# Attention, a Mish feed-forward and a routed mixture of experts: score products of two heads in turn, one half-sequence ahead

## The chip, the cores and the metric

The kernel runs on one core of a Trainium2 chip. The metric is the device time of one launch in microseconds (us). TensorE multiplies matrices, VectorE, ScalarE and GpSimd work on elements (GpSimd is POOL in the profile, VectorE DVE, ScalarE ACT), and SyncE (SP) issues most of the DMAs. The time before is the median of three runs.

## The reference

```python
scores = scale * np.matmul(q, k.transpose(0, 1, 3, 2))   # 4 x 8 heads, 576 x 576, head size 64
scores = np.where(masks[None], scores, -1e9)              # heads 0-3: the last 32 keys
                                                          # heads 4-7: every 4th of the last 128
attn = np.exp(scores - scores.max(-1, keepdims=True))
attn = attn / (attn.sum(-1, keepdims=True) + 1e-09)
x = np.matmul(attn, v)                                    # -> 2304 tokens x 512
h = x @ w_in                                              # 512 x 2048
sp = np.where(h > 20.0, h, np.log1p(np.exp(np.minimum(h, 20.0))))
x = (h * np.tanh(sp)) @ w_out                             # Mish, 2048 x 512
# every token goes to one of 8 experts (argmax of x @ w_gate):
# out = gate_w * sigmoid(x @ w_output_gate)[e] * relu(x @ w1[e]) @ w2[e]
```

The feed-forward weights w_in and w_out arrive as 8-byte floats and are made into 4-byte floats on the chip. Products that need more than one TensorE pass of reduced precision are made from a high and a low part of each operand (hi and lo, three products).

## The kernel before

The 2304 tokens are eight half-sequences (halves) j = 0 to 7 of 288 tokens; even ones are the first half of a sequence, odd ones the second.

**Attention of a half** goes by four pairs of heads p. Queries and keys of a pair lie with the one head's 64 dimensions in partitions 0 to 63 and the other's in 64 to 127. `att_b(j, p, h)` makes the masked scores of one head h in one PSUM bank (three blocks of 96 queries x 128 keys for the near heads, four of 72 x 72 or 72 x 104 for the dilated ones; L219), takes the row maximum (L226), the exponentials with their sums (ScalarE, L229), and multiplies each block by the reciprocal of its sums (L239). `att_c` transposes the probabilities (L250) and copies them out, `att_d` multiplies them with the values of both heads, alternating (L268), and splits the result into xhi (ScalarE, L274) and xlo (VectorE, L275), the input of the feed-forward. An fp32 product counts as two passes in the trace.

**PSUM** has eight banks: `ps_acc` with four (the feed-forward's sums acc), `ps_h` with two (hps) and `ps_a` with two, in turn. For j below EARLY = 2 scores and outputs use ps_acc and only transposes ps_a; later halves use ps_a for all three. There the mask is added when VectorE takes the scores out (L225); for the first two halves TensorE writes it into the bank (L213) and the queries are scaled beforehand (L212).

**The feed-forward** runs in 128 steps g, each for one half and 128 of the 2048 inner columns: `l1` (12 products hps, L408), Mish in `mish_a` to `mish_d`, and three steps later `l2` (12 products into the four banks acc, L451). Steps 0 to 31 take halves 0 and 1 in turn, four steps each; then come 16 steps for each half. Mish is made from exp(min(h, 20)): VectorE clamps out of PSUM (L415), ScalarE takes the exponential (L416), the square is on ScalarE (L418) for g below 32 and on VectorE (L420) later, ScalarE takes a logarithm (L426) and an exponential (L427), and VectorE multiplies with h (L432). `split` writes the high part on ScalarE (L352) and subtracts it for the low part (L354).

**Weights**: of each of the 32 pieces VectorE makes 4-byte floats in three instructions (`narrow`: L343, L345, L347), then `split` follows. During steps 0 to 31 the pieces come just ahead of their use. Of the subtractions, GpSimd does those of the weights, those of glo for g below 32, and those of x2s, the routing's input (four for each half).

**Order.** The source order sets each engine's queue, with priorities that let a scheduler move work; every engine then works its queue strictly in order, waiting by semaphores. Ahead of the loop of steps stands the attention of halves 0 and 1 (`att_first`), with three short filler products (`busy`, L92) behind each operation. The attention of half j + 1 is spread over the 16 steps of half j from j = 2 on (`take`), that of half 2 from step 22. The gate weights `wg` are loaded at the start (`setup_b`) and split at step 18. After step 127 come the experts.

Of the kernel before, what the change touches and what calls it, by code (L numbers as in the profile page):

```python
# [22 lines left out]
EPS = 1e-9  # L23
# [5 lines left out]
def tile_attn_mish_moe(ctx, tc, qkv, w_in, w_out, w_gate, w_og, w1, w2, out):  # L29
# [54 lines left out]
    two5 = const.tile([128, 2], F32, name="two5")  # L84
# [24 lines left out]
    def setup_b():  # L109
# [14 lines left out]
        nc.sync.dma_start(out=wg[:, :, 0:E], in_=w_gate.rearrange("(k p) e -> p k e", p=128))  # L124
        nc.sync.dma_start(out=wg[:, :, E:2 * E], in_=w_og.rearrange("(k p) e -> p k e", p=128))
# [23 lines left out]
    EARLY = 2  # L149
# [11 lines left out]
    scq = [wp.tile([128, 4096], F32, tag="w", name="scq") for _ in range(EARLY)]  # L161
# [3 lines left out]
    def early(tag, m, *shape):  # L165

        off, size, n = dict(pr=(0, 416, 4), pt=(1664, 288, 3))[tag]
# [3 lines left out]
        names = "abc"[:len(shape)]  # L171
        return t.rearrange(f"p ({' '.join(names)}) -> p {' '.join(names)}", **dict(zip(names, shape)))
# [24 lines left out]
    def att_b(j, p, h):  # L197
# [4 lines left out]
        hp = slice(64 * h, 64 * h + 64)  # L202
        n, m, w = (3, CH, 128) if p < 2 else (DIL, NP, NP + 32 * s)
        sc = banks(j, "s", [m, n, w], "sc")
# [4 lines left out]
        first = j < EARLY  # L209
        if first:  # L210
            if h == 0:
                nc.vector.tensor_scalar(out=qT, in0=qT, scalar1=D ** -0.5, scalar2=None, op0=ALU.mult)  # L212
            nc.tensor.matmul(out=sc, lhsT=idb[0:m, 0:m], rhs=mk, start=True, stop=False, skip_group_check=True)  # L213
        for u in range(n):
            if p < 2:
                a, c = qT[hp, CH * u:CH * u + CH], kT[hp, CH * u:CH * u + 128]
            else:
                a, c = qT[hp, NP * u:NP * u + NP], kT[hp, u, 32 - 32 * s:]
            nc.tensor.matmul(out=sc[:, u, :], lhsT=a, rhs=c, start=not first, stop=True, skip_group_check=True)  # L219
        nm = ap.tile([CH, 4], F32, tag="nm", name="nm", bufs=4)  # L220
        if first:
            pr, src = early("pr", m, n, w), sc
        else:
            pr = src = ap.tile([m, n, w], F32, tag="pr", name="pr", bufs=3)
            nc.vector.scalar_tensor_tensor(out=pr, in0=sc, scalar=D ** -0.5, in1=mk, op0=ALU.mult, op1=ALU.add)  # L225
        nc.vector.tensor_reduce(out=nm[0:m, 0:n], in_=src, op=ALU.max, axis=AX.X, negate=True)  # L226
        su = ap.tile([CH, 4], F32, tag="su", name="su", bufs=4)
        for u in range(n):
            nc.scalar.activation(out=pr[:, u, :], in_=src[:, u, :], func=AF.Exp, bias=nm[0:m, u:u + 1],  # L229
                                 accum_out=su[0:m, u:u + 1])  # L230
        nc.vector.tensor_scalar(out=su[0:m, 0:n], in0=su[0:m, 0:n], scalar1=EPS, scalar2=None, op0=ALU.add)
        nc.vector.reciprocal(out=su[0:m, 0:n], in_=su[0:m, 0:n])
        for u in range(n):
            x, scale = pr[:, u, :], su[0:m, u:u + 1]
            if first and u == 3:
                nc.scalar.activation(out=x, in_=x, func=AF.Copy, scale=scale)
            else:
                eng = nc.gpsimd if (j, u) == (0, 2) else nc.vector
                eng.tensor_scalar(out=x, in0=x, scalar1=scale, scalar2=None, op0=ALU.mult)  # L239
        st["p", h] = pr  # L240

    def att_c(j, p, h):
# [6 lines left out]
        for u in range(n):
            nc.tensor.transpose(tp[:, u, :], pr[:, u, :], idn[0:m, 0:m])  # L250
        pt = early("pt", w, n, m) if j < EARLY else ap.tile([w, n, m], F32, tag="pt", name="pt")
        if h == 0:
            nc.vector.tensor_copy(pt, tp)
        else:
            nc.scalar.activation(out=pt, in_=tp, func=AF.Copy)
        st["t", h] = pt
# [669 lines left out]
    if True:  # L926
# [228 lines left out]
```

## Time and profile before

| | us |
|---|---|
| median of three runs | 872.98 (871.68 to 880.41) |
| profiled execution | 870.95 |
| its span, first to last instruction | 869.2 |
| TensorE busy | 829.0 (95%) |
| VectorE busy | 587.0 (68%) |
| ScalarE busy | 509.1 (59%) |
| GpSimd busy | 201.4 (23%) |
| first l1 product of step 32 starts | 186.4 |
| first l1 product of step 112 (last half) starts | 531.4 |
| last l2 product of the feed-forward ends | 597.2 |

Busy times of different engines lie beside one another. The share of 95% is an average: the chain of work that ended last goes through TensorE for 71% of the span, VectorE for 13%, DMA and ScalarE for 4% each. So the stretches have to be read one by one. The times of single instructions of TensorE overlap their neighbours; what a group costs is read from starts.

### The profile page before, as it was taken

Reading aid. Unit: us, or ns where it says so; the run is one execution under the profiler, and the core shown is the slowest. Engines: PE = TensorE matmul, PEld = TensorE weight load, DVE = VectorE, ACT = ScalarE, POOL = GpSimd, SP = SyncE. Lnnn points to the kernel's source line nnn. Section 1 sums busy time; section 2 is a strip of 40 time slices with the busy share of each in tenths; the row PEclk is TensorE's granted clock in tenths of the full one; section 3 lists DMA queues with packets and bytes.
Section 4 is the critical chain, followed back from the end, with each engine's and each line's share of the span. In section 5 each row is a group of like instructions: output and inputs, shape, how many; then the busy total and the mean of one; then the engine's idle time right before and its main releaser. Section 6 shows DMA issues by size and latency. Waiting matters only on the chain.

```text
span 869.2 us, 16857 instructions
## 1 busy us (share of the span) xinstructions
PE 829.0 (95%) x6151; PEld 767.1 (88%) x6151; DVE 587.0 (68%) x1630; ACT 509.1 (59%) x1427; POOL 201.4 (23%) x201
## 2 busy tenths in 40 slices
PE   7988889999999999999999999989899999999994
PEld 5877879898999999999999999889789999999993
DVE  5799898968768767777777776785484526534510
ACT  3586657876667666666666666583463525545621
POOL 3326554332101001001010110251221313123300
PEclk6899999999999999999999999999999999999998
DMA  9541548511210210120121000240684526436300
GB/s 330 180 142 56 166 163 260 157 54 30 78 43 12 67 39 29 39 66 29 31 65 39 31 28 1 85 163 22 213 276 156 194 65 227 144 135 244 121 23 18
DMA packets 39841, 91.72 MB, mean 106 GB/s; under 512 B 4643, under 2 KB 12835, under 8 KB 39756
## 3 DMA queue, kind: packets, MB, share of 16 engines
q1 hardware_dynamic: 36508, 81.16, 28.8%
q0 software_dynamic: 3248, 9.46, 3.3%
q8 instruction: 49, 0.80, 0.4%
q14 instruction: 36, 0.29, 0.1%
HBM read 73.91 MB, written 17.41 MB: 105 GB/s over the span
## 4 chain that ended last, share of the span: by engine, by line
PE 71%; DVE 13%; issue 6%; DMA 4%; ACT 4%; POOL 1%; SPq 1%; POOLq 0%; ACTq 0%; DVEq 0%
PE hps L408 20%; PE acc L451 19%; PE eh L750 8%; PE ecol L784 6%; PE sc L219 6%; DMA est<-in_moe_w_dram 3%; PE eacc L792 2%; PE o L268 2%; DVE wf L345 2%; PE tp L250 2%; DVE we L354 2%; DVE wf L343 2%; DVE wf L347 1%; ACT we L352 1%; PE busy L92 1%
## 5 line engine op out<-in xcount | busy, mean ns | idle before, releaser
L408 PE MATMUL hps<-xhi,w 128*128 128x288 f32 x1024 | 243.1, 307 | 13.5 <-DVE e L432 12.1
L408 PEld LDWEIGHTS hps<-xhi,w 128*128 128x128 f32 x1024 | 174.8, 190 | 21.2 <-DVE e L432 15.9
L451 PE MATMUL acc<-ghi,w 128*128 128x288 f32 x1024 | 171.5, 303 | 3.2 <-ACT x2T L471 2.0
L408 PE MATMUL hps<-xlo,w 128*128 128x288 f32 x512 | 153.0, 299 | 0.5
L451 PEld LDWEIGHTS acc<-ghi,w 128*128 128x128 f32 x1024 | 145.6, 190 | 8.5 <-ACT x2T L471 2.2
L750 PE MATMUL eh<-exh,we 128*128 128x256 f32 (+5 forms) x448 | 108.6, 316 | 0.0
L408 PEld LDWEIGHTS hps<-xlo,w 128*128 128x128 f32 x512 | 97.9, 191 | 2.0 <-DVE xlo L275 1.9
L352 ACT ACTIVATE we<-est 128x512 fp32r<-128x512 f32 x128 | 74.5, 624 | 39.3 <-DMA est<-in_moe_w_dram 22.6
L416 ACT ACTIVATE e<-e 128x288 f32<-128x288 f32 x128 | 55.8, 437 | 64.1 <-DVE e L415 62.1
L451 PE MATMUL acc<-glo,w 128*128 128x288 f32 x512 | 89.3, 296 | 0.0
L354 DVE TENSOR_TENSOR we<-est,we 128x512 fp32r<-128x512 f32 x92 | 69.2, 786 | 28.3 <-ACT we L352 28.1
L352 ACT ACTIVATE ghi<-e 128x288 fp32r<-128x288 f32 x128 | 56.5, 442 | 44.9 <-PE acc L451 24.4
L354 POOL TENSOR_TENSOR we<-est,we 128x512 fp32r<-128x512 f32 x36 | 49.6, 1398 | 131.2 <-ACT we L352 131.0
L426 ACT ACTIVATE e<-e,two 128x288 f32<-128x288 f32 x128 | 67.8, 530 | 20.7 <-DVE e L420 20.2
L415 DVE TENSOR_SCALAR e<-hps 128x288 f32<-128x288 f32 x128 | 57.9, 452 | 31.9 <-PE hps L408 30.5
L750 PEld LDWEIGHTS eh<-exh,we 128*128 128x128 f32 x448 | 77.1, 188 | 1.3
L451 PEld LDWEIGHTS acc<-glo,w 128*128 128x128 f32 x512 | 75.4, 189 | 0.0
L755 DVE SCALAR_TENSOR_TENSOR eg<-eh,eg 128x256 fp32r<-128x256 f32 (+5 forms) x64 | 30.9, 483 | 61.7 <-ACT eg L754 61.5
L229 ACT ACTIVATE pr<-pr,nm 96x128 f32<-96x128 f32 (+2 forms) x168 | 61.9, 370 | 16.7 <-DVE nm L226 16.5
L750 PE MATMUL eh<-exl,we 128*128 128x256 f32 (+5 forms) x224 | 69.7, 311 | 0.0
L432 DVE SCALAR_TENSOR_TENSOR e<-e,hps 128x288 f32<-128x288 f32 x128 | 56.9, 444 | 14.4 <-ACT e L427 14.1
L784 PE MATMUL ecol<-eg,we 128*128 128x440 f32 (+3 forms) x384 | 65.4, 320 | 0.5 <-DVE eg L755 0.5
(196 smaller groups left out, 1469.4 us busy)
## 6 DMA issues: line engine op xcount, KB each, us to landing
est<-in_moe_w_dram SPq DMA_DIRECT2D x64, 512.0 KB
wst<-in_moe_w_in_dram SPq DMA_DIRECT2D x16, 512.0 KB
wst<-in_moe_w_out_dram SPq DMA_DIRECT2D x16, 512.0 KB
qkv<-in_qkv_dram SPq DMA_DIRECT2D x12, 608.0 KB
qkv<-in_qkv_dram SPq DMA_DIRECT2D x14, 496.0 KB
buf<-fill SPq DMA_DIRECT2D x8, 771.0 KB
xs<-buf SPq DMA_DIRECT2D x19, 257.0 KB
scq<-in_qkv_dram SPq DMA_DIRECT2D x4, 608.0 KB
```

The costliest lines, as they stand in the source:

```text
L219: nc.tensor.matmul(out=sc[:, u, :], lhsT=a, rhs=c, start=not first, stop=True, skip_group_check=True)
L229: nc.scalar.activation(out=pr[:, u, :], in_=src[:, u, :], func=AF.Exp, bias=nm[0:m, u:u + 1], accum_out=su[0:m, u:u + 1])
L352: nc.scalar.activation(out=hi, in_=src, func=AF.Copy)
L354: eng.tensor_tensor(out=lo, in0=src, in1=hi.bitcast(F32), op=ALU.subtract)
L408: nc.tensor.matmul(out=hps[g], lhsT=w[:, a, kk, 128 * fl:128 * fl + 128], rhs=(xhi, xlo)[x][j][:, kk, :], start=(kk == 0 and n == 0), stop ...
L415: nc.vector.tensor_scalar(out=e, in0=hps[g], scalar1=20.0, scalar2=None, op0=ALU.min)
L416: nc.scalar.activation(out=e, in_=e, func=AF.Exp)
L426: nc.scalar.activation(out=r, in_=r, func=AF.Ln, scale=0.2, bias=two5[:, 1:2] if g < 2 * NF else two5[:, 0:1])
L432: nc.vector.scalar_tensor_tensor(out=u, in0=u, scalar=2.5, in1=hps.pop(g), op0=ALU.subtract, op1=ALU.mult)
L451: nc.tensor.matmul(out=accs[j][m], lhsT=w[:, a, fl, 128 * m:128 * m + 128], rhs=gg[x], start=(first and n == 0), stop=(last and n == 2))
L750: nc.tensor.matmul(out=ps, lhsT=ew[q, 0, a][:, c:c + 128], rhs=(hi, lo)[x][:, kk, 0:n], start=(k == 0), stop=(k == 3 * KD - 1))
L784: nc.tensor.matmul(out=accs["e", q][k], lhsT=ew[q, 1, a][:, c:c + 128], rhs=gg[x], start=(f == 0 and n == 0), stop=(f == NF2 - 1 and n == 2))
```

## The change

- Only half 0's attention stands ahead of the steps (EARLY = 1), with 30 and then 12 filler products behind each operation. Half 1's is taken in steps 0 to 3 and uses the two banks of ps_a for scores, transposes and outputs; its mask is still written by TensorE (PEMASK = 2).
- `att_s` makes the scores of both heads of a pair, block by block in turn, into two banks. Sums, reciprocals and the multiplication are done once for a pair; the multiplication is one VectorE instruction with two tensor operands. The scaling of the queries goes from VectorE to GpSimd.
- `split` subtracts on VectorE, but for the experts' pieces that were on GpSimd.
- Mish takes the exponential straight from PSUM; VectorE then limits it to e^20 and adds 1, from SBUF to SBUF.
- The gate weights are loaded at step 12, not at the start.

```diff
@@ setup
-        nc.sync.dma_start(out=wg[:, :, 0:E], in_=w_gate.rearrange("(k p) e -> p k e", p=128))
-        nc.sync.dma_start(out=wg[:, :, E:2 * E], in_=w_og.rearrange("(k p) e -> p k e", p=128))
-    EARLY = 2
+    EARLY = 1
+    PEMASK = 2
...
-    def att_b(j, p, h):
+    def att_s(j, p):
...
-        sc = banks(j, "s", [m, n, w], "sc")
+        sc = [banks(j, "s", [m, n, w], "sc") for _ in range(2)]
...
-        first = j < EARLY
+        first = j < PEMASK
         if first:
-            if h == 0:
-                nc.vector.tensor_scalar(out=qT, in0=qT, scalar1=D ** -0.5, scalar2=None, op0=ALU.mult)
-            nc.tensor.matmul(out=sc, lhsT=idb[0:m, 0:m], rhs=mk, start=True, stop=False, skip_group_check=True)
+            nc.gpsimd.tensor_scalar(out=qT, in0=qT, scalar1=D ** -0.5, scalar2=None, op0=ALU.mult)
+            for h in range(2):
+                nc.tensor.matmul(out=sc[h], lhsT=idb[0:m, 0:m], rhs=mk, start=True, stop=False, skip_group_check=True)
         for u in range(n):
...
-            nc.tensor.matmul(out=sc[:, u, :], lhsT=a, rhs=c, start=not first, stop=True, skip_group_check=True)
+            for h in range(2):
+                hp = slice(64 * h, 64 * h + 64)
...
+                nc.tensor.matmul(out=sc[h][:, u, :], lhsT=a, rhs=c, start=not first, stop=True, skip_group_check=True)
...
-        for u in range(n):
-            x, scale = pr[:, u, :], su[0:m, u:u + 1]
-            if first and u == 3:
-                nc.scalar.activation(out=x, in_=x, func=AF.Copy, scale=scale)
-            else:
-                eng = nc.gpsimd if (j, u) == (0, 2) else nc.vector
-                eng.tensor_scalar(out=x, in0=x, scalar1=scale, scalar2=None, op0=ALU.mult)
+        nc.vector.tensor_tensor(out=pr, in0=pr, in1=x.unsqueeze(3).to_broadcast([m, 2, n, w]), op=ALU.mult)
...
-        split(hi, lo, narrow(t) if wide else t, True)
+        split(hi, lo, narrow(t) if wide else t)
...
-        nc.vector.tensor_scalar(out=e, in0=hps[g], scalar1=20.0, scalar2=None, op0=ALU.min)
-        nc.scalar.activation(out=e, in_=e, func=AF.Exp)
+        nc.scalar.activation(out=e, in_=hps[g], func=AF.Exp)
+        nc.vector.tensor_scalar(out=e, in0=e, scalar1=math.exp(20.0), scalar2=1.0, op0=ALU.min, op1=ALU.add)
         if g < 2 * NF:
-            nc.scalar.activation(out=e, in_=e, func=AF.Square, bias=1.0)
+            nc.scalar.activation(out=e, in_=e, func=AF.Square)
         else:
-            nc.vector.scalar_tensor_tensor(out=e, in0=e, scalar=2.0, in1=e, op0=ALU.add, op1=ALU.mult)
+            nc.vector.tensor_tensor(out=e, in0=e, in1=e, op=ALU.mult)
...
-        split(hi, lo, u, g < 2 * NF)
+        split(hi, lo, u)
...
-            split(hi[:, m, :], lo[:, m, :], x2[:, m, :], True)
+            split(hi[:, m, :], lo[:, m, :], x2[:, m, :])
...
-        for i, op in enumerate(att_first()):
+        busy(30, warm, 128)
+        for i, op in enumerate(attention(0)):
             op()
-            busy(3, idb, 128)
-            if i == 4:
+            busy(12, idb, 128)
+            if i == 2:
                 setup_b()
...
-        begin = {THIRD: (2, 2 * NF)}
+        begin = {0: (1, 4), THIRD: (2, 2 * NF)}
...
+            if g == FILLS - 6:
+                nc.sync.dma_start(out=wg[:, :, 0:E], in_=w_gate.rearrange("(k p) e -> p k e", p=128))
+                nc.sync.dma_start(out=wg[:, :, E:2 * E], in_=w_og.rearrange("(k p) e -> p k e", p=128))
```

Three places of the engines' queues show what moves. The first is TensorE in the steps of the later halves: before, the two score groups of one pair of heads (sc, from the pair's loaded queries and keys qkv) stand apart, each at a place of its own between feed-forward products.

```order
L451 MATMUL acc_4676<-glo_5338,w_1800 128x288
L219 MATMUL sc_5447<-qkv_5302 96x128 x3
L408 MATMUL hps_5464<-xhi_4785,w_266 128x288
...
L451 MATMUL acc_4675<-ghi_5380,w_1800 128x288 x2
L219 MATMUL sc_5492<-qkv_5302 96x128 x3
L451 MATMUL acc_4676<-ghi_5380,w_1800 128x288 x2
```

Now a pair's six products stand together and alternate between the two banks. All pairs of halves 3 to 7 stand like this.

```order
L388 MATMUL hps_5233<-xhi_4585,w_291 128x288
L218 MATMUL sc_5251<-qkv_4589 96x128
L218 MATMUL sc_5252<-qkv_4589 96x128
L218 MATMUL sc_5251<-qkv_4589 96x128
L218 MATMUL sc_5252<-qkv_4589 96x128
L218 MATMUL sc_5251<-qkv_4589 96x128
L218 MATMUL sc_5252<-qkv_4589 96x128
L431 MATMUL acc_4494<-ghi_5166,w_1762 128x288 x2
```

The second place is TensorE at the second pair of half 1 (its queries and keys lie in scq_113; idb is the identity that writes the mask). Before, fillers stand between the two heads' scores.

```order
L213 MATMUL sc_554<-mask_99,idb_98 96x384
L219 MATMUL sc_554<-scq_113 96x128 x3
L92 LDWEIGHTS idb_98
L92 MATMUL busy_571<-idb_98 128x128
...
L213 LDWEIGHTS idb_98
L213 MATMUL sc_575<-mask_99,idb_98 96x384
L219 MATMUL sc_575<-scq_113 96x128 x3
```

Now they stand among the products of the first steps, one head behind the other, and the transposes of the pair before, which take the next bank of ps_a, follow at once.

```order
L388 MATMUL hps_660<-xhi_320,w_291 128x288
L210 LDWEIGHTS idb_98
L210 MATMUL sc_635<-mask_99,idb_98 96x384
L218 MATMUL sc_635<-scq_113 96x128 x3
L210 LDWEIGHTS idb_98
L210 MATMUL sc_636<-mask_99,idb_98 96x384
L218 MATMUL sc_636<-scq_113 96x128 x3
L246 MATMUL tp_667<-idn_97,pr_621 128x96 x3
L388 MATMUL hps_746<-xhi_320,w_291 128x288
```

The third is the cast of the gate weights (wgs) on ScalarE. Before, it is that queue's first real instruction.

```order
L927 ACT_TABLE_LOAD
L352 ACTIVATE wgs_108<-wg_107 128x4x16
L229 ACTIVATE scr_111,su_155<-sc_147,nm_153 96x128 x3
L229 ACTIVATE scr_111,su_175<-sc_168,nm_173 96x128 x3
L352 ACTIVATE w_266<-wf_267 128x4x128
```

Now it stands in the first steps, ahead of the exponentials of half 1's third pair (pr_724) and behind a Mish exponential.

```order
L332 ACTIVATE ghi_787<-e_686 128x288
L395 ACTIVATE e_772<-hps_746 128x288
L332 ACTIVATE wgs_108<-wg_107 128x4x16
L229 ACTIVATE pr_724,su_723<-sc_709,nm_722 72x104 x4
L398 ACTIVATE e_772<-e_772 128x288
L229 ACTIVATE pr_724,su_723<-sc_710,nm_722 72x104 x4
```

## Rows read from the trace of the kernel before

**Rows 1.** Windows: us, then busy us of each engine, clock, DMA share, GB/s.

```profile
0.00:186.40 186.40, 166.31 (x1297) 146.69 (x1297) 158.22 (x387) 124.38 (x398) 86.45 (x93) 0.93 0.53 172
186.40:531.40 345.00, 344.19 (x2773) 321.63 (x2771) 259.67 (x851) 225.01 (x695) 33.94 (x40) 1.00 0.14 42
531.40:869.20 337.80, 318.53 (x2088) 298.78 (x2085) 169.15 (x392) 159.68 (x336) 81.03 (x69) 0.99 0.41 134
```

**Rows 2.** Timeline, TensorE, from 346 us: start, us, what.

```profile
345.99 0.69 PE L451 MATMUL acc<-glo,w 128*128 128x288 f32 x4
346.61 0.89 PE L219 MATMUL sc<-qkv 64*96 64x128 f32 x6
347.43 0.40 PE L408 MATMUL hps<-xhi,w 128*128 128x288 f32 x1
347.66 0.29 PE L408 MATMUL hps<-xlo,w 128*128 128x288 f32 x1
347.80 0.43 PE L408 MATMUL hps<-xhi,w 128*128 128x288 f32 x2
...
349.13 0.95 PE L451 MATMUL acc<-ghi,w 128*128 128x288 f32 x6
350.01 0.72 PE L268 MATMUL o<-pt,qkv 128*64 128x96 f32 x12
350.65 0.53 PE L451 MATMUL acc<-ghi,w 128*128 128x288 f32 x2
```

**Rows 3.** Lines, VectorE, 0 to 186.4: busy us, mean ns | idle before, releaser.

```profile
L345 DVE SCALAR_TENSOR_TENSOR wf<-wst,wf 128x512 int32<-128x512 int32 x32 | 30.8, 969 | 0.2
L347 DVE SCALAR_TENSOR_TENSOR wf<-wst,wf 128x512 int32<-128x512 int32 x32 | 27.6, 873 | 0.2
L343 DVE TENSOR_SCALAR wf<-wst 128x512 int32<-128x512 int32 x32 | 21.5, 681 | 1.2 <-POOL w L354 1.2
L415 DVE TENSOR_SCALAR e<-hps 128x288 f32<-128x288 f32 x32 | 14.4, 449 | 5.1 <-PE hps L408 4.7
...
L239 DVE TENSOR_SCALAR scr<-scr,su 96x128 f32<-96x128 f32 (+2 forms) x40 | 10.3, 306 | 0.0
...
L239 DVE TENSOR_SCALAR pr<-pr,su 72x72 f32<-72x72 f32 (+1 forms) x28 | 7.7, 332 | 0.1
...
L212 DVE TENSOR_SCALAR scq<-scq 128x288 f32<-128x288 f32 x6 | 1.8, 300 | 2.9 <-DMA scq<-in_qkv_dram 2.9
```

**Rows 4.** Lines, GpSimd, 0 to 186.4.

```profile
L354 POOL TENSOR_TENSOR w<-wf,w 128x512 fp32r<-128x512 f32 x32 | 45.1, 1416 | 20.2 <-ACT w L352 19.8
```

**Rows 5.** Timeline, VectorE: two conversions without GpSimd, one beside it.

```profile
31.89 0.75 DVE L343 TENSOR_SCALAR wf<-wst 128x512 int32<-128x512 int32 x2
...
32.62 0.68 DVE L345 SCALAR_TENSOR_TENSOR wf<-wst,wf 128x512 int32<-128x512 int32 x1
...
63.34 1.77 DVE L345 SCALAR_TENSOR_TENSOR wf<-wst,wf 128x512 int32<-128x512 int32 x1
```

**Rows 6.** Lines, TensorE, 0 to 186.4.

```profile
L408 PE MATMUL hps<-xhi,w 128*128 128x288 f32 x257 | 61.6, 314 | 10.4 <-DVE e L432 9.2 <-POOL w L354 1.2
```

**Rows 7.** Lines, VectorE, 186.4 to 531.4.

```profile
L354 DVE TENSOR_TENSOR glo<-e,ghi 128x288 fp32r<-128x288 f32 x79 | 35.8, 454 | 11.6 <-PE acc L451 6.8 <-ACT ghi L352 3.9
...
L225 DVE SCALAR_TENSOR_TENSOR pr<-sc,mask 96x384 f32<-96x384 f32 (+2 forms) x40 | 21.7, 542 | 8.5 <-PE sc L219 7.6 <-issue 0.6
```

**Rows 8.** Timeline, half 1's second pair: mask product, last sum of exponentials.

```profile
39.78 0.33 PE L213 MATMUL sc<-mask,idb 96*96 96x384 bf16 x1
...
45.22 0.21 ACT L229 ACTIVATION_READ_ACCUMULATOR scr<-sc,nm 96x1 f32 x1
```

**Rows 9.** Lines by form, TensorE, 186.4 to 531.4: the score products.

```profile
L219 PE MATMUL sc<-qkv 64*96 64x128 f32 x120 | 17.8, 282 | 0.0
L219 PE MATMUL sc<-qkv 64*72 64x104 f32 x96 | 11.2, 256 | 0.0
...
L219 PE MATMUL sc<-qkv 64*72 64x72 f32 x64 | 5.9, 232 | 0.0
```

More of the change, by code (lines that the diff above doesn't have):

```diff
@@ L83, in tile_attn_mish_moe @@
     wgs = const.tile([128, KD, 4 * E], F32R, name="wgs")
-    two5 = const.tile([128, 2], F32, name="two5")
+    two5 = const.tile([128, 1], F32, name="two5")
     cum = const.tile([CH, E], BF16, name="cum")
@@ L160, in tile_attn_mish_moe @@
     scr = wp.tile([128, 4096], F32, tag="w", name="scr")
-    scq = [wp.tile([128, 4096], F32, tag="w", name="scq") for _ in range(EARLY)]
+    scq = [wp.tile([128, 4096], F32, tag="w", name="scq") for _ in range(2)]
     wst2 = wp.tile([128, 4096], F32, tag="w", name="wst2")
@@ L165, in early @@
     def early(tag, m, *shape):
-        off, size, n = dict(pr=(0, 416, 4), pt=(1664, 288, 3))[tag]
+        off, size, n = dict(pr=(0, 832, 3), pt=(2496, 288, 3))[tag]
         i = rot[tag] = rot.get(tag, -1) + 1
@@ L182, in load @@
         n = 992 if p < 2 else 1216
-        if j < EARLY and p:
+        if j < 2 and p:
             off = 992 + 1216 * (p - 2) if p > 1 else 0
@@ L226, in att_b @@
-        nc.vector.tensor_reduce(out=nm[0:m, 0:n], in_=src, op=ALU.max, axis=AX.X, negate=True)
-        su = ap.tile([CH, 4], F32, tag="su", name="su", bufs=4)
-        for u in range(n):
[L229 to L232, printed above, removed]
@@ new lines, in att_s @@
+        nm = ap.tile([CH, 2, 4], F32, tag="nm", name="nm", bufs=2)
+        su = ap.tile([CH, 2, 4], F32, tag="su", name="su", bufs=2)
+        pr = early("pr", m, 2, n, w) if j < EARLY else ap.tile([m, 2, n, w], F32, tag="pr", name="pr", bufs=2)
+        for h in range(2):
+            src = sc[h]
+            if not first:
+                src = pr[:, h]
+                nc.vector.scalar_tensor_tensor(out=src, in0=sc[h], scalar=D ** -0.5, in1=mk, op0=ALU.mult, op1=ALU.add)
+            nc.vector.tensor_reduce(out=nm[0:m, h, 0:n], in_=src, op=ALU.max, axis=AX.X, negate=True)
+            for u in range(n):
+                nc.scalar.activation(out=pr[:, h, u, :], in_=src[:, u, :], func=AF.Exp, bias=nm[0:m, h, u:u + 1],
+                                     accum_out=su[0:m, h, u:u + 1])
@@ L244, in att_c @@
+        x = su[0:m, :, 0:n]
+        nc.vector.tensor_scalar(out=x, in0=x, scalar1=EPS, scalar2=None, op0=ALU.add)
+        nc.vector.reciprocal(out=x, in_=x)
+        nc.vector.tensor_tensor(out=pr, in0=pr, in1=x.unsqueeze(3).to_broadcast([m, 2, n, w]), op=ALU.mult)
+        st["p"] = pr
+    def att_c(j, p):
         s = j % 2
         st = state[j, p]
-        pr = st.pop(("p", h))
+        pr = st.pop("p")
         n, m, w = (3, CH, 128) if p < 2 else (DIL, NP, NP + 32 * s)
-        tp = banks(j, "t", [w, n, m], "tp")
@@ L249, in att_c @@
[L249 to L256, printed above, removed]
+        for h in range(2):
+            tp = banks(j, "t", [w, n, m], "tp")
+            for u in range(n):
+                nc.tensor.transpose(tp[:, u, :], pr[:, h, u, :], idn[0:m, 0:m])
+            pt = early("pt", w, n, m) if j < EARLY else ap.tile([w, n, m], F32, tag="pt", name="pt")
+            if h == 0:
+                nc.vector.tensor_copy(pt, tp)
+            else:
+                nc.scalar.activation(out=pt, in_=tp, func=AF.Copy)
+            st["t", h] = pt
@@ L425, in mish_b @@
         r = mt[g]
-        nc.scalar.activation(out=r, in_=r, func=AF.Ln, scale=0.2, bias=two5[:, 1:2] if g < 2 * NF else two5[:, 0:1])
+        nc.scalar.activation(out=r, in_=r, func=AF.Ln, scale=0.2, bias=two5)
         nc.scalar.activation(out=r, in_=r, func=AF.Exp, scale=-1.0)
@@ L933, in tile_attn_mish_moe @@
         setup_a()
-        for i, op in enumerate(att_first()):
-            op()
-            busy(3, idb, 128)
-            if i == 4:
+        busy(30, warm, 128)
+        for i, op in enumerate(attention(0)):
+            op()
+            busy(12, idb, 128)
+            if i == 2:
                 setup_b()
+                w_to(2, 400)
+                for _ in range(4):
+                    next_load()
             if i == 6:
-                for _ in range(4 * EARLY - 4):
-                    next_load()
-            if i >= 3:
-                w_to(min(UPFRONT, (i - 1) // 4), 400)
-        for _ in range(2):
-            next_load()
+                w_to(4, 400)
         first = []
```

47 lines of the change are left out of this document (11 added, 36 removed).

## The prediction

> **What bounds the kernel now.** I read the windows view first, cut where the first third ends [rows 1]. From 186.4 to 531.4 us TensorE is busy for 344.2 of 345.0 us at full clock while VectorE is busy for 259.7: this stretch ends when TensorE has done its products, and only fewer or shorter TensorE groups shorten it. From 0 to 186.4 us it is the other way round in part: TensorE is busy for 166.3 us (with some filler products in that), VectorE for 158.2, GpSimd for 86.5, and the mean granted clock is 0.93. After 531.4 us TensorE is busy for 318.5 of 337.8 us; there the change touches next to nothing. So three sums are wanted, early, middle and late.
>
> In the middle the timeline of TensorE shows what a group of score products costs [rows 2]. The reader should take starts only, as ends overlap. Six feed-forward products in a row take 0.95 us and one alone 0.29, so a further one costs (0.95 - 0.29)/5 = 0.132 us. Between the start of the four acc products (345.99) and that of the fifth product behind them (347.80) lie 1.81 us, of which six products are 0.79; the score group of one head, six passes, costs the other 1.02. The output group of twelve passes, whose heads alternate in the two column halves, costs 350.65 - 349.13 - 6 x 0.132 = 0.73. Passes that use only half of the array can thus run beside each other in this kernel, at least by columns, and the score groups do not do so.
>
> Early, the lines of VectorE show the conversions: 32 pieces, 0.969 + 0.873 + 0.681 us on the mean for their three instructions, half of VectorE's work [rows 3]. GpSimd's subtraction takes 1.416 us a piece [rows 4]. The timeline shows what they do to each other [rows 5]: at 31.9 and 32.6 us, with GpSimd idle, two of the first instruction take 0.75 and one of the second 0.68; at 63.3 us, with GpSimd subtracting, one of the second takes 1.77. The waits behind TensorE's first products of a step are then mostly on VectorE's last Mish instruction, 9.2 of 10.4 us [rows 6].
>
> **The change, part by part.**
>
> *Subtractions on VectorE.* It removes GpSimd's share from the first third and so the slowing: 32 x (0.969 - 0.68) + 32 x (0.873 - 0.68) + 32 x (0.681 - 0.40) = 9.2 + 6.2 + 9.0 = 24 us of VectorE (0.40 is about half of the 0.75 pair; the third instruction, of the second's form, is taken at the second's 0.68). It adds 32 weight subtractions; two-input instructions of that size cost 0.68, so 21.8 us; 31 subtractions of glo at 0.454 as VectorE already does them later [rows 7], 14.1 us; and four of x2s, 1.8 us. Middle: x2s, 20 x 0.454 = 9 us more, covered by VectorE's 85 us of idleness.
>
> *Clamp after exp.* VectorE then reads and writes SBUF; 288 such columns take 0.300 in the prescale [rows 3] against 0.449 from PSUM: 32 x 0.15 = 5 us less early. ScalarE gets the same number of instructions. In the first 32 steps the square stays on ScalarE, so a step's chain crosses one engine more; later it crosses one less.
>
> *Merged softmax.* The multiplications are 40 + 28 of 10.3 + 7.7 = 18.0 us early. Twelve merged ones of 576 to 832 columns replace them; at a column per cycle (512 in 0.68) and a slow start they cost about 0.85, so 10 us: 8 less. The sum and reciprocal are done once a pair, about 2 less, and the prescale's 8 x 0.30 = 2.4 goes to GpSimd, which is now nearly empty.
>
> VectorE early: 158.2 - 24 - 5 - 8 - 2 - 2.4 + 21.8 + 14.1 + 1.8 = 154, 4 us less. The work hardly falls; the long instructions in front of the Mish chain do. I therefore count the 9.2 us of waits on it as gone too, and nothing for the shorter front, since the second half's attention now runs inside steps 0 to 3. Early: -13. Bounds: 0 if the waits only change their name; -26 if VectorE were never idle beyond some 6 us (154 + 6 = 160).
>
> *Second half's attention in two banks.* Before, a pair's banks are held from 39.78 to 45.43, 5.65 us [rows 8]; four pairs, 23 us, in a front that had filler products instead of waits. Now each pair holds both banks of ps_a, and transposes and outputs wait for them; TensorE's queue behind has feed-forward products that wait too. This is inside the early bounds.
>
> *Alternating score products.* Middle: 120, 96 and 64 rows are 20, 12 and 8 groups [rows 9]; by the same reading they cost 1.02, 1.06 and 0.87, together 40 us for 20 pairs. If two heads run beside each other, a pair costs one group: -20. If not, merging two groups saves only what is not passes (1.02 - 6 x 0.12, about 0.30) once a pair: -6. I take the first, by the output group: the same alternation, the nearest row. Against it stand new bank waits: after a pair's transposes little other work stands before the next user of the banks, and I set 0.2 us a pair, 4 us. Middle: -16, bounds -6 and -20. In three pairs of the second half and two of the third the scheduler has put the heads one behind the other again, so I count no pairing early.
>
> The page "TensorEngine Tiling (Array Packing)" of the Trainium skill, under Key Properties, says that different tiles can execute weight loads and products in parallel; Gotcha 1 asks for different banks, which the two heads have. The output rows agree for column halves; no row here shows it for row halves. By the page alone the middle would be -20.
>
> *Gate weights later.* Their cast stands in ScalarE's queue ahead of the exponentials of the second half's third pair, and their DMAs on SP behind four weight loads that wait for VectorE. Between 0 and 2 us, inside the early bounds; no gain, as TensorE did not wait for it.
>
> *Late:* 0, +-2.
>
> Sum: -13 - 16 = -29. The profiled execution took 870.95 us, so 842; the median of the runs is 2.0 above it, so 844 us.
>
> **Rivals.**
>
> *A, the forecast:* chance 0.60.
>
> *B, row halves do not run beside each other.* For it: no row shows them. Against: the output group. Middle -6, with the early gain 871 - 19 + 2 = 854 us. Chance 0.18.
>
> *C, the two banks become the bound (slower).* TensorE works strictly in order. If it reaches the next user of ps_a right behind a pair's scores, it waits for both mask-and-scale instructions (2 x 0.542) and for two 288-column instructions ahead of them (2 x 0.454) [rows 7]: 2.0 us a pair, 24 pairs, 48 us, of which 4 are counted: 844 + 44 = 888 us. It decides from (29 + 4)/24 = 1.4 us a pair. For it: one head held one bank before, now a pair holds both. Against: in the order thirty feed-forward products, 30 x 0.132 = 4.0 us, stand between one pair's scores and the next pair's. Chance 0.06.
>
> *D, the early third comes down to VectorE's sum,* -26: 844 - 13 = 831 us; with no bank waits in the middle 827. Chance 0.10.
>
> *E, the merged multiplication is slow and takes the early gain.* Rows: a small one costs 0.25 to 0.35 for 72 to 128 columns, mostly a fixed price, so merging pays. If instead a merged one took twice a column's rate of the small ones' form, 1.5 us each, VectorE would have +8 instead of -8 early, 154 would be 170, and the early gain nil: 857 us. Chance 0.06. The page "VectorE: DVE Perf Modes" of the Trainium skill, section "Mode 2×_2P", says that fp32 tensor_scalar from SBUF can use both read ports while tensor_tensor cannot. The pair at 31.9 (about 0.40) against 0.68 behind it agrees on the rates; by the rates alone the edit would lose, and the small rows' fixed price speaks against that.
>
> **How the numbers follow.** Forecast and D end at least 1% faster, B and E too by the centre, though some of B and E lies within 1% (864 to 882, about what a measurement can tell from no change). Faster 0.84, same 0.10 (edges of B and E, and half-sized C), slower 0.06. The range leaves out 2 in 10: below, half of D; above, C and the worse edge of B and E with no early gain: 844 - 18 = 826 to 844 + 20 = 864, the latter being middle -6 and early about -3.
>
> **What would show it.** Windows of the profile after: the stretch of the later halves' steps shorter by about 16 us with TensorE still full; a pair's twelve score passes taking about 1.0 us between starts, not 1.7. Conversions at 0.40, 0.68 and 0.68. Waits on the last Mish instruction below 3 us in the first 32 steps. Wrong would be: TensorE idle ahead of transposes, outputs or scores in sum above 10 us (C), or the early third as long as before.

## The result, and the profile after

The changed kernel takes 846.7 us (median of four runs, 844.5 to 848.7) against 872.5 for the kernel before: ratio 0.968, 95% interval 0.962 to 0.975. The forecast was 844. The profiled execution took 846.0 us with a span of 844.3, 24.9 less than before.

The windows view of the changed kernel, cut where its step 32 and its step 112 start (columns as in [rows 1]), says where they come from.

```profile
0.00:176.20 176.20, 159.62 (x1351) 143.26 (x1352) 149.97 (x365) 122.45 (x390) 10.59 (x26) 0.94 0.57 183
176.20:507.60 331.40, 327.60 (x2773) 309.81 (x2771) 237.91 (x713) 220.55 (x695) 16.74 (x18) 0.99 0.14 43
507.60:844.30 336.70, 318.57 (x2087) 298.81 (x2085) 170.37 (x396) 158.81 (x336) 78.13 (x65) 0.99 0.40 135
```

Against [rows 1] the first third is 10.2 us shorter (forecast 13), the middle 13.6 (forecast 16), the rest 1.1. VectorE's sum in the first third fell from 158.2 to 150.0, but its idle time only from 28.2 to 26.2. In the middle TensorE is no longer quite full: 3.8 us idle where there were 0.8.

The score products of a pair, timeline of TensorE after, answer to [rows 2]:

```profile
317.64 0.29 PE L388 MATMUL hps<-xhi,w 128*128 128x288 f32 x1
317.87 0.90 PE L218 MATMUL sc<-qkv 64*96 64x128 f32 x12
318.69 1.33 PE L431 MATMUL acc<-ghi,w 128*128 128x288 f32 x8
319.86 0.43 PE L431 MATMUL acc<-glo,w 128*128 128x288 f32 x2
```

From 317.64 to 319.86 lie 2.22 us, nine feed-forward products of them 9 x 0.132 = 1.19: both heads together cost 1.03 us, what one head cost before.

VectorE's lines up to step 32, after, answer to [rows 3, 7]:

```profile
L334 DVE TENSOR_TENSOR w<-wf,w 128x512 fp32r<-128x512 f32 x32 | 21.8, 682 | 0.0
L327 DVE SCALAR_TENSOR_TENSOR wf<-wst,wf 128x512 int32<-128x512 int32 x32 | 21.8, 681 | 0.0
L325 DVE SCALAR_TENSOR_TENSOR wf<-wst,wf 128x512 int32<-128x512 int32 x32 | 21.7, 683 | 0.1
...
L334 DVE TENSOR_TENSOR glo<-e,ghi 128x288 fp32r<-128x288 f32 x30 | 13.5, 451 | 0.5 <-ACT e L398 0.4
L323 DVE TENSOR_SCALAR wf<-wst 128x512 int32<-128x512 int32 x32 | 13.2, 416 | 4.8 <-DMA wst<-in_moe_w_in_dram 4.8
L396 DVE TENSOR_SCALAR e<-e 128x288 f32<-128x288 f32 x32 | 9.6, 300 | 1.2 <-ACT e L395 1.0
...
L234 DVE TENSOR_TENSOR pr<-pr,su 96x768 f32<-96x768 f32 (+2 forms) x8 | 7.3, 912 | 0.0
...
L234 DVE TENSOR_TENSOR scr<-scr,su 96x768 f32<-96x768 f32 (+1 forms) x4 | 3.4, 846 | 0.0
```

The conversions run at 0.42, 0.68 and 0.68 us (forecast 0.40, 0.68, 0.68), the clamp at 0.300. New is VectorE's 4.8 us of waiting for weights. What TensorE waits for there (view of waits, 0 to 176.2 us: total, times, longest) answers to [rows 6]:

```profile
PE acc L431 <- DVE glo L334: 3.1, 1, 3.1
PE hps L388 <- DVE e L412: 2.8, 4, 1.3
PE tp L246 <- DVE scr L234: 2.7, 1, 2.7
PE sc L210 <- ACT pr L229: 1.9, 1, 1.9
PE tp L246 <- DVE pr L234: 1.6, 1, 1.6
```

The waits on the last Mish instruction (L412) fell from 9.2 to 2.8 us as forecast. Others took their place: a low part behind late weights (L431), a transpose in the front that waits for the merged multiplication (scr), and in steps 0 to 2 the two banks (L210, and L246 with pr).

### The profile page after: what moved, and what is told of

It is laid out like the page before. It is cut to its first block, busy times and chain, and to the rows that moved or that the text cites. A ratio compares the mean times of both kernels' runs of the same rounds, so it can differ in the third digit from the quotient of the medians.

```text
span 844.3 us, 16623 instructions
## 1 busy us (share of the span) xinstructions
PE 805.8 (95%) x6205; PEld 751.9 (89%) x6205; DVE 558.3 (66%) x1473; ACT 501.8 (59%) x1419; POOL 105.5 (12%) x109
## 4 chain that ended last, share of the span: by engine, by line
PE 68%; DVE 12%; DMA 6%; issue 5%; ACT 5%; POOL 1%; SPq 1%; POOLq 0%; ACTq 0%; DVEq 0%
PE hps L388 20%; PE acc L431 19%; PE eh L730 8%; PE ecol L764 6%; DMA wst<-in_moe_w_in_dram 3%; PE o L264 3%; DMA est<-in_moe_w_dram 3%; PE eacc L772 2%; PE sc L218 2%; ACT pr L229 2%; PE tp L246 2%; DVE we L334 2%; ACT we L332 1%; DVE pr L226 1%; DVE nm L227 1%
## 5 line engine op out<-in xcount | busy, mean ns | idle before, releaser
L388 PE MATMUL hps<-xhi,w 128*128 128x288 f32 x1024 | 239.7, 306 | 6.4 <-DVE e L412 6.2
L388 PEld LDWEIGHTS hps<-xhi,w 128*128 128x128 f32 x1024 | 175.2, 191 | 11.7 <-DVE e L412 7.0
L431 PE MATMUL acc<-ghi,w 128*128 128x288 f32 x1024 | 172.5, 302 | 2.3 <-DVE x2T L449 1.3
L431 PEld LDWEIGHTS acc<-ghi,w 128*128 128x128 f32 x1024 | 145.9, 190 | 8.1 <-DVE x2T L449 2.3
L431 PE MATMUL acc<-glo,w 128*128 128x288 f32 x512 | 92.8, 297 | 3.1 <-DVE glo L334 3.1
L332 ACT ACTIVATE we<-est 128x512 fp32r<-128x512 f32 x128 | 74.4, 624 | 33.3 <-PE eh L730 16.4
L395 ACT ACTIVATE e<-hps 128x288 f32<-128x288 f32 x128 | 51.6, 404 | 55.0 <-PE hps L388 55.0
L334 DVE TENSOR_TENSOR we<-est,we 128x512 fp32r<-128x512 f32 x92 | 66.1, 755 | 25.2 <-ACT we L332 25.2
L431 PEld LDWEIGHTS acc<-glo,w 128*128 128x128 f32 x512 | 76.6, 190 | 3.7 <-DVE glo L334 3.4
L582 POOL DMA_INDIRECT buf<-row,si x24 | 22.5, 936 | 417.5 <-DVE si L547 245.4
L334 DVE TENSOR_TENSOR glo<-e,ghi 128x288 fp32r<-128x288 f32 x128 | 59.1, 462 | 20.1 <-PE acc L431 10.5
L412 DVE SCALAR_TENSOR_TENSOR e<-e,hps 128x288 f32<-128x288 f32 x128 | 57.4, 448 | 22.1 <-ACT e L407 21.8
## 6 DMA issues: line engine op xcount, KB each, us to landing
scq<-in_qkv_dram SPq DMA_DIRECT2D x4, 608.0 KB, 10.2
```

The lines of the kernel that those rows point to most:

```text
L332: nc.scalar.activation(out=hi, in_=src, func=AF.Copy)
L334: eng.tensor_tensor(out=lo, in0=src, in1=hi.bitcast(F32), op=ALU.subtract)
L388: nc.tensor.matmul(out=hps[g], lhsT=w[:, a, kk, 128 * fl:128 * fl + 128], rhs=(xhi, xlo)[x][j][:, kk, :], start=(kk == 0 and n == 0), stop ...
L395: nc.scalar.activation(out=e, in_=hps[g], func=AF.Exp)
L412: nc.vector.scalar_tensor_tensor(out=u, in0=u, scalar=2.5, in1=hps.pop(g), op0=ALU.subtract, op1=ALU.mult)
L431: nc.tensor.matmul(out=accs[j][m], lhsT=w[:, a, fl, 128 * m:128 * m + 128], rhs=gg[x], start=(first and n == 0), stop=(last and n == 2))
```

## The experiments

All times are medians. The kernel before, run beside each of them, stood at 871.7 to 873.3. Since totals mix the stretches, this table gives starts of steps (first hps product, us) from the profiled executions; "48 to 112" is the stretch in which only the steady work of halves 3 to 6 and the attention of 4 to 7 run.

| kernel | us | step 4 | 10 | 22 | 32 | 48 to 112 |
|---|---|---|---|---|---|---|
| before | 872.5 | 66.6 | 94.5 | 140.8 | 186.4 | 273.1 |
| changed | 846.7 | 60.7 | 85.2 | 124.4 | 176.2 | 259.7 |
| e1 heads one behind the other | 844.0 | 56.7 | 80.4 | 118.6 | 168.7 | 263.2 |
| e2 GpSimd subtracts | 864.6 | 65.2 | 97.1 | 143.8 | 187.9 | 265.7 |
| e3 fills earlier | 845.7 | 59.2 | 83.3 | 122.5 | 172.1 | 259.6 |
| e4 two halves ahead | 838.4 | 58.0 | 77.5 | 116.7 | 168.5 | 259.6 |
| e5 only the subtractions | 875.4 | 74.4 | 92.1 | 138.0 | 197.0 | 272.1 |
| e6 old clamp | 848.2 | 64.8 | 89.7 | 129.9 | 182.8 | 259.1 |
| e7 small multiplications | 847.1 | 54.1 | 87.3 | 126.8 | 179.8 | 258.3 |
| e8 two ahead, spread | 835.2 | 57.3 | 76.8 | 122.3 | 166.9 | 259.5 |
| e9 heads at two places | 851.8 | 55.0 | 78.3 | 119.0 | 171.5 | 270.6 |
| e10 e8, one behind the other | 844.7 | 63.1 | 82.2 | 128.4 | 173.0 | 263.2 |

**e1, alternation undone.**

```diff
-        for u in range(n):
-            for h in range(2):
+        for h in range(2):
+            for u in range(n):
```

> The changed kernel with the score products of a pair's two heads one behind the other (all blocks of head 0, then all of head 1), nothing else. Theory: the middle's gain is the alternation. A pair's group, 1.02 us between starts in the changed kernel, becomes 12 passes x 0.12 + 0.30 = 1.74 us; 20 pairs x 0.72 = 14 us more between step 32 and step 112, so about 861 us and the middle at 345 us again. Rival: the gain comes from fewer groups (each entry paid once a pair), and the order inside a group does nothing: 847 us, group 1.02.

844.0 us (841.5 to 847.1), no slower than the change. The time is nearer the rival's, but the group is neither's: the timeline of TensorE in this kernel shows it at 1.33 us (313.12 to 315.51, less 8 x 0.132):

```profile
313.12 0.96 PE L431 MATMUL acc<-ghi,w 128*128 128x288 f32 x6
314.01 1.19 PE L218 MATMUL sc<-qkv 64*96 64x128 f32 x12
315.14 0.54 PE L431 MATMUL acc<-ghi,w 128*128 128x288 f32 x2
315.51 0.70 PE L431 MATMUL acc<-glo,w 128*128 128x288 f32 x4
```

That is neither 1.74 nor 1.02. By their spacing in the trace the six passes of head 0 start at 314.01, .20, .31, .42, .53 and .64, those of head 1 at 314.32, .50, .61, .72, .83 and .94: the second head starts behind the third pass of the first, and the rest runs beside it. So row halves do run beside each other, and TensorE finds part of that by itself when the heads merely stand together. From step 48 to 112 the alternation is worth 263.2 - 259.7 = 3.5 us; e10 against e8 gives 3.7. In e1 the first third happens to be 7.5 us shorter, which hides it; 4.0 of that stand ahead of step 4. Such a difference is not yet an edit's: the kernels with one half ahead and the change's subtractions (changed, e1, e3, e6, e7, e9) start step 4 at anything from 54.1 to 64.8 us, with granted clocks of 0.74 to 1.00 from their first step to step 4.

**e9, heads at two places** (halves 2 to 7; the sums and the multiplication stay merged). `att_s` makes one head's scores there; halves 0 and 1 do so for both heads in a row, so their heads stand one behind the other.

```diff
-            if p < 4:
-                ops.append(lambda p=p: att_s(j, p))
+            if p < 4 and j < 2:
+                ops.append(lambda p=p: (att_s(j, p, 0), att_s(j, p, 1)))
+            elif p < 4:
+                ops.append(lambda p=p: att_s(j, p, 0))
             if p > 0:
                 ops.append(lambda p=p: att_c(j, p - 1))
+            if p < 4 and j >= 2:
+                ops.append(lambda p=p: att_s(j, p, 1))
...
```

> The changed kernel with the scores of a pair's two heads made at two places of the order again for halves 2 to 7 (halves 0 and 1 as changed); sums and multiplication stay merged. Theory: the middle's gain is that the heads stand together, so that one head's passes run beside the other's; apart, each head's group costs 1.02 us, a pair 2.0 instead of 1.0, and with smaller transposes' cost unchanged the middle is 12 to 16 us longer (343 to 347 us), the time 858 to 864 us. Rival: the middle's gain comes from the subtractions of x2s and the fewer operations per half, since the order inside a group (heads one behind the other) cost nothing: 846 to 851 us.

851.8 us (850.5 to 853.0); from step 48 to 112, 270.6 against 259.7. The theory holds in kind; the total is lower than its range because the first third is 4.7 us shorter and steps 32 to 47, with half 3's attention, do not get longer (70.4 against 71.8). The middle now adds up for 16 pairs: everything else in the change 273.1 to 270.6 (-2.5), the heads together 270.6 to 263.2 (-7.4), in turn 263.2 to 259.7 (-3.5).

**e2, GpSimd subtracts again.**

```diff
-        split(hi, lo, narrow(t) if wide else t)
+        split(hi, lo, narrow(t) if wide else t, True)
...
-        split(hi, lo, u)
+        split(hi, lo, u, g < 2 * NF)
...
-            split(hi[:, m, :], lo[:, m, :], x2[:, m, :])
+            split(hi[:, m, :], lo[:, m, :], x2[:, m, :], True)
```

> The changed kernel with the subtractions of the weights, of glo in steps 0 to 31 and of x2s on GpSimd again. Theory: GpSimd's subtractions slow VectorE's conversions; the three instructions go from 0.41, 0.68, 0.68 back to about 0.7, 0.97, 0.87 us, waits on the last Mish instruction return in steps 4 to 21 (63.7 us in the changed kernel, 74 before), and the time is 855 to 860 us. Rival: the early gain comes from the shorter front and the merged softmax, and VectorE with 36 us less of its own work makes up for the slowing: 844 to 849 us.

864.6 us (863.4 to 867.5), 18 more than the change: the theory in kind, but beyond its range. Of these, 11.7 us lie up to step 32 and 6.0 from step 48 to 112, where only x2s is on GpSimd: there TensorE waits 3.8 us for VectorE's x2T and 1.7 us for the last Mish instruction, against 1.3 us and none in the changed kernel. The kernel before, also with x2s on GpSimd, shows neither wait there, so these 6 us are no gain of the change over it. VectorE's lines up to step 32 in this kernel:

```profile
L325 DVE SCALAR_TENSOR_TENSOR wf<-wst,wf 128x512 int32<-128x512 int32 x32 | 28.2, 883 | 0.2
L327 DVE SCALAR_TENSOR_TENSOR wf<-wst,wf 128x512 int32<-128x512 int32 x32 | 27.3, 859 | 0.1
L323 DVE TENSOR_SCALAR wf<-wst 128x512 int32<-128x512 int32 x32 | 19.9, 628 | 0.9 <-DMA wst<-in_moe_w_in_dram 0.9
L396 DVE TENSOR_SCALAR e<-e 128x288 f32<-128x288 f32 x32 | 17.9, 562 | 3.6 <-ACT e L395 3.5
...
L234 DVE TENSOR_TENSOR pr<-pr,su 96x768 f32<-96x768 f32 (+2 forms) x8 | 10.1, 1263 | 0.0
```

Beside GpSimd not only the conversions are slow: the new clamp takes 0.562 us instead of 0.300, more than the old one out of PSUM (0.449, [rows 3]), and the merged multiplication 1.263 instead of 0.912. So the new clamp gains only with GpSimd quiet. The merged multiplications gain either way: beside GpSimd all twelve take 14.5 us, where the small ones of [rows 3] take 18.0.

**e5, the subtractions alone**, in the kernel before (the same three lines, the other way).

> The kernel before with one part of the change alone: all subtractions of the feed-forward's split on VectorE, none on GpSimd. Theory: this part needs the others, which make room on VectorE. Alone VectorE's sum up to step 32 is 158 - 24 + 38 = 172 us, so that third cannot shrink below about 176 us from 186, and most of that only if the waits go: 864 to 871 us. Rival: taking GpSimd away is the whole early gain by itself, since undoing it cost the changed kernel 18 us: 853 to 858 us.

875.4 us (869.6 to 878.9), ratio 0.999 (0.995 to 1.003): nothing, and the theory was still too kind. Windows up to step 32 of e5 (its profile is of its longest run, 3.5 us above the median) and of e2:

```profile
0.00:197.00 197.00, 178.17 (x1308) 156.37 (x1308) 161.86 (x453) 127.48 (x396) 9.28 (x26) 0.88 0.50 163
```

```profile
0.00:187.90 187.90, 165.52 (x1350) 145.78 (x1351) 151.57 (x299) 122.19 (x392) 91.89 (x92) 0.93 0.51 171
```

Neither half of the change shortens the first third (197.0 and 187.9 against 186.4); both together do (176.2). By stretches e5 is not nothing, though. Steps 4 to 21 take 63.6 us, against 74.2 before, 63.7 in the changed kernel and 78.6 in e2: there the subtractions alone make the gain. e5 loses it elsewhere, 7.8 us up to step 4 and 13.4 us in steps 22 to 31, where VectorE is busy for 50.3 of 59.0 us.

**e6, Mish as before** (the removed lines of the diff put back).

> The changed kernel with Mish as before (VectorE clamps out of PSUM at about 0.45 us, then the exponential). Theory: VectorE has 32 x 0.15 = 5 us more to do up to step 32, where it is busy 95% of the time, and nothing changes later: 849 to 852 us. Rival: the step's chain crosses one engine fewer in the first 32 steps, and that makes up for it: 844 to 848 us.

848.2 us (842.3 to 849.2). VectorE's clamp is back at 0.453 us, its sum up to step 32 is 155.3 us instead of 150.0, and step 32 is 6.6 us later; but the next 16 steps give 2.5 back, and the runs overlap with the change's. The medians are 1.5 us apart and do not tell the two apart.

**e7, one multiplication for each block.**

```diff
-        nc.vector.tensor_tensor(out=pr, in0=pr, in1=x.unsqueeze(3).to_broadcast([m, 2, n, w]), op=ALU.mult)
+        for h in range(2):
+            for u in range(n):
+                nc.vector.tensor_scalar(out=pr[:, h, u, :], in0=pr[:, h, u, :], scalar1=su[0:m, h, u:u + 1],
+                                        scalar2=None, op0=ALU.mult)
```

> The changed kernel with the softmax multiplication as six or eight one-block instructions with a scalar operand instead of one instruction with two tensor operands. Theory: the merged one takes 0.74 to 0.94 us, the small ones 6 x 0.35 or 8 x 0.25 = 2.0 us; 12 pairs up to step 32 give VectorE 13 us more there, so 852 to 860 us, and the wait of a transpose on the multiplication (2.0 us at 43.9) gets longer. Rival: by the rates of the two forms the small ones are not slower: 844 to 848 us.

847.1 us (846.8 to 848.0): no difference, the rival's outcome. Up to step 32 the 56 small ones take 10.9 us where eight merged ones take 7.3 (with half 0's, 16.3 against 10.7). Their records last 0.264 us but overlap: in a row they start every 0.167 to 0.196 us, and the theory priced them by the records. GpSimd is a smaller part of it: the small ones of [rows 3], 18.0 us, take 14.5 in e5, with next to no GpSimd beside them. VectorE's sum up to step 32 is 155.9 us instead of 150.0; the time does not show it.

**e3, the fills earlier.**

```diff
-            if FILLS <= g < FILLS + E:
-                setup_rows(g - FILLS)
+            if 4 <= g < 4 + 2 * E and g % 2 == 0:
+                setup_rows((g - 4) // 2)
```

> The changed kernel with the zero-fill DMAs of the routing buffer (eight of 771 KB and eight of 112 KB) put at every second step from step 4, not at steps 18 to 25. Theory: steps 22 to 31 lost 6 us against before because the fills fill the DMA queues (busy share 1.00 from 135 to 148 us) and a weight piece comes late: TensorE idle 4.9 us at 147.9 to 152.9 and then 5.4 us at half clock. Without it the time is about 839 us (838 to 842), with the clock at 1.00 in steps 22 to 31. Rival: VectorE is the bound there (busy 10.5 of 10.6 and 11.8 of 12.9 us), the piece's wait only hides it: 845 to 847 us.

845.7 us (842.1 to 846.2). This was the question of steps 22 to 31, which the change made longer (51.8 against 45.6). Windows of the changed kernel there:

```profile
124.40:147.86 23.46, 22.50 (x187) 20.52 (x186) 22.31 (x55) 18.20 (x65) 0.00 (x0) 1.00 0.98 287
147.86:152.94 5.08, 0.69 (x5) 0.28 (x3) 3.71 (x8) 1.77 (x4) 0.00 (x0) 0.91 0.92 248
152.94:158.00 5.06, 5.06 (x21) 5.06 (x22) 3.47 (x10) 2.77 (x7) 0.00 (x0) 0.50 0.58 172
```

TensorE stands for 4.4 us and then works at a granted clock of 0.50, the lower level (1.2 GHz). On VectorE's timeline the piece behind it is 2.14 us late:

```profile
146.40 0.68 DVE L325 SCALAR_TENSOR_TENSOR wf<-wst,wf 128x512 int32<-128x512 int32 x1
149.22 0.43 DVE L323 TENSOR_SCALAR wf<-wst 128x512 int32<-128x512 int32 x1 [2.14 <-DMA wst<-in_moe_w_in_dram]
```

With the fills gone the DMA share in this stretch falls from 0.63 to 0.33, and TensorE's standstill is one of 2.0 us. Steps 22 to 31 still take 49.6 us with VectorE busy for 45.7: the fills were about 2 of the 6 us, and the rival is nearer for the rest. e2 bears it out: with the subtractions on GpSimd, steps 22 to 31 take 44.1 us with VectorE busy for 35.4.

**e4, two halves ahead.**

```diff
-    EARLY = 1
+    EARLY = 2
...
-        busy(30, warm, 128)
-        for i, op in enumerate(attention(0)):
+        front = []
+        for i in range(9):
+            if i < 8:
+                front.append(lambda i=i: att_s(*tasks[i]))
+            if i >= 1:
+                front.append(lambda i=i: att_c(*tasks[i - 1]))
+                front.append(lambda i=i: att_d(*tasks[i - 1]))
+        for i, op in enumerate(front):
             op()
-            busy(12, idb, 128)
+            busy(5, idb, 128)
...
-        begin = {0: (1, 4), THIRD: (2, 2 * NF)}
+        begin = {THIRD: (2, 2 * NF)}
```

The loads and the weight pieces of the front are moved along with it.

> The changed kernel with both first halves' attention ahead of the steps again (scores and outputs of half 1 in the four banks of ps_acc, five fillers behind each operation), the rest as changed. Theory: only one half ahead brings step 4 forward by about 6 us (60.7 against 66.6), so this kernel takes 851 to 854 us. Rival: the two banks for half 1's attention cost as much as the overlap brings (steps 0 to 3 take 33 us for 12.7 us of products): 843 to 848 us.

838.4 us (837.0 to 839.9), 8 less than the change: the theory was wrong in sign, and the rival outdone. One half ahead brought nothing that two halves ahead do not. How much it costs, if anything, is less sure than the total says: e1, with one half ahead, reaches step 32 as early (168.7). At step 10 the kernels with two ahead stand at 76.8 to 82.2, those with one ahead and the change's VectorE work (changed, e1, e3, e9) at 78.3 to 85.2; about 3 us on the mean, with ranges that overlap.

**e8 and e10, spread.** e8 is e4 with the fills of e3 and `THIRD = 18`; e10 is e8 with the loop order of e1.

> Two halves ahead as in the kernel of that name, the zero fills at every second step from step 4, and half 2's attention spread over steps 18 to 31 instead of 22 to 31. Theory: VectorE's load in steps 22 to 31 is the bound there (46 of 52 us with a weight piece late), spreading it over four more steps and freeing the DMA queues takes 3 to 6 us off 838: 832 to 836 us. Rival: VectorE is as full in steps 4 to 21 (60.5 of 63.7 us), so the work only moves: 837 to 841 us.

> The kernel with two halves ahead and spread work, with the score products of a pair's heads one behind the other. Theory: one behind the other still runs half beside each other, 1.35 us a pair against 1.01, and this is given back in the neighbouring transposes, so 834 to 838 us. Rival: without the disturbance by the first steps' order the alternation shows its 20 x 0.34 = 7 us: 840 to 843 us.

e8 takes 835.2 us (833.9 to 835.8), ratio 0.954 (0.947 to 0.961), and beats both kernels. The reason given for it failed: steps 10 to 31 take 90.1 us against 91.0 in e4, so the work moved, as the rival has it (45.5 and 44.6 instead of 39.2 and 51.8). The rest of the 3 us lies in the front (0.7) and in steps 32 to 47 (1.9). e10 takes 844.7 (841.7 to 847.3): nearer the rival than the theory. Of the 9.5 us to e8, 3.7 are the alternation and 6.1 stand in the first third. The granted clock of the front differs, with the same work (windows of e8, of e10 and, in two pieces, of e4):

```profile
0.00:23.80 23.80, 16.54 (x109) 10.85 (x109) 13.84 (x47) 8.09 (x34) 10.93 (x25) 1.00 0.90 333
```

```profile
0.00:23.80 23.80, 16.01 (x98) 10.76 (x99) 13.77 (x46) 7.92 (x33) 10.66 (x25) 0.67 0.90 332
```

```profile
10.00:20.00 10.00, 4.36 (x32) 3.19 (x28) 9.48 (x20) 5.70 (x27) 4.07 (x3) 0.50 1.05 395
20.00:24.40 4.40, 4.40 (x42) 3.73 (x40) 2.80 (x7) 1.76 (x10) 1.01 (x2) 0.50 0.83 293
```

But that is not the 6.1 us: e4 works at 0.50 from 10.0 to 24.4 us and starts step 4 only 0.7 us behind e8. What e10 loses, it loses in steps 0 to 3 (38.0 us at a granted clock of 0.91, against 33.5 at 1.00). What tips the clock in either place these runs do not settle.

## Why the prediction was right

**Alternating products: right, and mechanism right.** A pair costs 1.03 us, the forecast one group, and rival B fell. Score groups fell by half, as the sum had it. The term was sized for 20 pairs less 4 us of bank waits, -16; measured -13.6. The 16 pairs from step 48 on brought 13.4, half 3's four nothing: 71.9 and 71.8 us. Read by starts as in [rows 2] and summed from step 48 to 112, the score groups alone cost 31.6 us before, 31.5 in e9, 21.2 in e1 and 15.9 in the changed kernel. That is the forecast's one group for each of the 16 pairs; some 2 us of it were lost again beside them, 1.3 in waits of TensorE for VectorE's x2T that the kernel before does not have. In half 3's steps the forecast's bank wait stands once, and large:

```profile
206.19 0.40 PE L218 MATMUL sc<-qkv 64*72 64x104 f32 x2
208.52 0.93 PE L218 MATMUL sc<-qkv 64*72 64x104 f32 x14 [1.93 <-ACT lgT L484]
```

The second head's bank was held by the routing logits, whose ScalarE copy waited 4.2 us for the routing's indirect DMA; the clock then falls to 0.72 and 0.82 until 216 us. This is rival C's mechanism at one place, not at 24; in the other kernels that take turns there, the same steps take 69.3 to 71.6 us. The argument missed that heads standing together already bring two thirds of the gain (7.4 of 10.9 us). One reading was uneven: the output group's 0.73 was taken to the next product's start, the score group's 1.02 to the one after; read alike the output group costs 0.84. It was a sign of parallel passes all the same.

**First third: the size nearly right (-10.2 for -13), in part by luck.** VectorE's sum fell by 8.2 us, not 4, and the waits on Mish fell about as priced (-6.4 of 9.2). Where they stood, in steps 4 to 21, the stretch is 10.5 us shorter: the term did there what the forecast says (the waits on Mish fell from 9.2 to 1.0 us), and e5 and e2 show that it is the subtractions. But the step "I count the 9.2 us of waits as gone" let nothing take their place, and the front was counted at nothing. Measured, the part up to step 4 is 5.9 us shorter and steps 22 to 31 are 6.2 longer; that these two nearly cancel is luck. The 6.2 are in the main VectorE's, which now subtracts there too (e2 takes them back), and about 2 the zero fills' (e3), by a weight piece that comes late: TensorE waits 3.1 us for its low part, then works at half clock. The 5.9 stay open: step 4 of kernels with one half ahead varies by more than that.

**Subtractions on VectorE: right in size, wrong as a term by itself.** The slowing was 9 + 6 + 8 us as worked out, but e5 and e2 show no gain in the first third from either half alone. A sum over the whole third hid that the same edit shortens steps 4 to 21 and lengthens steps 22 to 31, where VectorE needs the room that the other parts make. That the other parts help by this room is argued from VectorE's busy time; no run adds them to e5 one at a time.

**Clamp and merged softmax: right in VectorE's time, little of it in the run's.** Priced at -5 and -8 us of VectorE, they took off 4.8 (14.4 to 9.6) and 7.3 (18.0 to 10.7). Undone one at a time they move the time by 1.5 and 0.4 us, within the spread of the runs (e6, e7). Rival E is not borne out: merged 10.7 us, small 16.3. Its sum was wrong too: twelve at 1.5 us are 18.0, as much as the small ones of [rows 3], so VectorE's 8 us would be lost (162), not 16 (170).

**One half ahead: counted at nothing, and it brought nothing; it may have cost.** e4 puts this at up to 8 us, the starts of step 10 at about 3 with overlapping ranges. The prescale, moved to GpSimd, takes 0.952 to 1.302 us there instead of 0.300, at the head of each of the first pairs:

```profile
L208 POOL TENSOR_SCALAR scq<-scq 128x288 f32<-128x288 f32 x6 | 5.7, 952 | 1.9 <-DMA scq<-in_qkv_dram 1.7
L208 POOL TENSOR_SCALAR qkv<-qkv 128x288 f32<-128x288 f32 x2 | 2.6, 1302 | 10.6 <-DMA qkv<-in_qkv_dram 10.6
```

Whether this costs time was not tried. It is not what sets the change apart from e4, which scales on GpSimd too.

## What to carry to other kernels

A price in an engine's busy time is not yet a price in time: the clamp and the merged multiplication took 5 and 7 us off VectorE as forecast, and undoing either moved the time by no more than 1 to 2. Before pricing an edit, look what ran beside its rows: the clamp from SBUF beats the one from PSUM only with GpSimd quiet. Products of 64 rows gain first from standing next to their partner, and a little more from taking turns. Where order decides, compare kernels by stretches: the changed kernel and e1 differed by 7.5 us in the first third, though only the order of a few products sets them apart there, while the stretch from step 48 to 112 told apart 3.5; and misses in two stretches can cancel in a total.

## What the runs showed of the hardware

- TensorE runs passes on the two row halves beside each other even in block order: by the spacing of the starts in e1 the second head starts behind the third pass of the first, 1.33 us for twelve passes against 1.03 in turn and 2 x 1.02 apart.
- VectorE's instructions that read and write only SBUF are slower on the mean where GpSimd subtracts (e2 against the change): the 288-column clamp from 0.300 to 0.562 us, the merged multiplication from 0.912 to 1.263, the conversions from 0.68 to 0.86 and 0.88 on the mean. Those that read PSUM are not: the Mish product 0.446 and 0.447, the old clamp 0.453 without GpSimd (e6) and 0.449 beside it [rows 3].
- The granted clock in the first 24 us was 0.67 in e10 and 1.00 in e8, and 0.50 from 10 to 24 us in e4, with the same work in nearly the same order; e4 and e8 still start step 4 within 0.7 us of each other.
